# Two PSUM banks for the second layer's output instead of one, in a fused attention and mixture-of-experts kernel

## The chip, the cores and the metric

One core of one Trainium2 chip runs the whole program. The time is the device time of one execution in microseconds (us); of several runs the median counts. The engines are named as the profile names them: PE multiplies matrices, ACT applies functions and copies with a scale, DVE and POOL work on vectors, SP issues most transfers; POOL also issues the scatters whose row addresses are data.

## What is computed

The reference, cut to what matters (4 batches of 11456 rows of 128 numbers, 49 agents, 8 experts with 1024 hidden units):

```python
def sm(a, b):
    s = scale * (a @ b.transpose(0, 2, 1))
    s = s - s.max(-1, keepdims=True)
    e = np.exp(s)
    return e / (e.sum(-1, keepdims=True) + 1e-09)
agent_v = sm(agents, k) @ v
x = (sm(q, agents) @ agent_v).reshape(B * N, 128)

logits = x @ w_gate                      # 45824 x 8
expert_idx = np.argmax(logits, axis=1)
gate_w = softmax(logits)[np.arange(B * N), expert_idx]
for e in range(8):
    rows = expert_idx == e
    y[rows] = np.maximum(x[rows] @ w1[e], 0.0) @ w2[e]
return gate_w[:, None] * y
```

## The kernel before, in words

**Stages.** For each batch, `k_ops` forms the scores of the 49 agents with all keys and their maximum, `v_ops` takes the exponentials and sums the values, which gives agent_v, and `m_ops` multiplies agent_v with each expert's w1 (L640), splits the product into a high and a low fp16 part (ACT at L645, DVE at L648) and stores it in DRAM as `md` (L653). So layer 1 of a token needs only its 49 probabilities: they multiply the 49 rows of `md`.

The 90 blocks of 128 queries of a batch are cut into groups (`GROUPS`, L72, 9 in all, of 16 to 50 blocks). For each group `q_ops` loads queries (`cf` buffers, L376), splits them (L380 on ACT, L384 on DVE), multiplies them with the agents (L399 to L401, into a PSUM tile `misc`), takes the exponentials into `rows` (L694 to L708), transposes them (L723, into `misc`, copied out by ACT at L728) and multiplies them for the router's logits (L737, copied out by ACT at L741). `r_ops` finds each token's expert and place (two matmuls at L800 and L804, the rest on DVE) and writes `tab`, which expert each tile of 128 tokens has (L937 to L960). `row_ops` lets POOL scatter each block of 128 rows to DRAM by place (L972, out is `rows`): one indirect transfer per block, 360 in all.

**Tiles.** `tile_ops` does the experts' part, 372 tiles of 128 tokens of one expert. Four tiles share a load of their rows (`ec` L1030, `rt` L1032). SP stages the tile's weights where the expert changes (`Mst` L1010, `Wst` L1006). PE does layer 1 (16 matmuls, L1041 and L1042) into the PSUM tile `hp`; ACT the relu into `hhi` (L1090); DVE the rest `hlo` (L1094); PE layer 2, 16 matmuls with `hhi` (L1048, L1049) and 8 with `hlo` (L1054), into the PSUM tile `yp`; ACT scales it into `yo` (L1105); POOL scatters the 128 rows to the output (L972, out is `out`). On PE the order is layer 1 of tile i+1, then layer 2 of tile i; on ACT the relu of tile i+1, then yo of tile i.

`w_ops` loads w2 of each expert once (L1138) and splits it into a high part (ACT, L1144) and a low part (DVE, L1147) in `w2s`. Some experts use the fixed load buffers `cf`, some the plain buffers `wf`, some a part of the score buffer S, as `W2CF` and `W2S` say. `m_ops` loads w1 of experts 4 to 6 of the first batch through `wf`.

**PSUM.** Its eight banks hold two `hp` tiles of two banks, three `misc` and one `yp`. `RINGS` (L79) says how many tiles or buffers each name has; a new one waits until the one that it takes the place of is read.

**The order.** Every piece of work is an `op` of `Plan` (L101 to L212) with an engine, a cost in us, a key (about its due time, counted in tiles; negative before the first tile) and what it depends on. `run` takes step by step the engine and the piece that could start first by the costs, then the one with the lowest key, and looks no further ahead than `WINDOW` (for SP, in the early part, `AHEAD0`) beyond the lowest key that is left. The instructions of each engine stand in that order. The constants near the top give keys: `KQ0`, `QK1`, `W1K`, `W2K`, `W2V`, `W2VD` and `PRE1` for the first two groups and the weights, `QAFTER` and `W2L` for behind which load of v a load may go, `R1K` for the row scatters of the second group, and `A2K`, `A3K`, `RATE2` and `RATE` for the start and length of the later groups:

```python
    a = A2K
    for g in GR[2:]:
        end = s0[g.i] - ENDK
        b = end - (RATE2 if g.b == 0 else RATE) * g.nb
...
        row_ops(g, Keys(b, end, g.nb))
        a = b
```

The layer-2 tile and its place in the ring of `yp`:

```python
            x.yp = ps.tile([P, P], F32, name="yp", bufs=RINGS["yp"])
            layer2_hi(x.yp, o, x.hi)
```

Of the kernel before, what the change touches and what calls it, by code (L numbers as in the profile page):

```python
# [41 lines left out]
NS = 4  # L42
SPARE = (2, 1, 1, 1)
CUT, CUT2, KPOOL, VPOOL = (0.18, 0.31, 0.44), 0.33, (), ()
R1K = (-17.6, -0.2)
RATE2, A3K = 0.46, -5.5
RATE = 1.085
ENDK = 8.6
WINDOW = 20.0
SLACK0, SLACK = 0.1, 0.08  # L50
AHEAD0 = 40.0
QK1, A2K = -910.0, -27.3
QAFTER = 3
KQ0 = -964.0
W2L = [8] * 8
W1L = [8] * 8
LDK = 3.3
PRE1 = -20.0
W2CF = (4, 5, 6, 7)

MMC0 = 1.85
FIRSTW, SK0 = 0.5, 900.0
# [1 line left out]
TABK0 = -944.5  # L64
MRING = ("mm", "mm", "mm", "hhi", "hhi", "hlo", "hlo", "mm")
W1S, W2S = (7,), (0, 1, 2)
MK, MKD, W2V, W2VD = -947.5, 0.02, -947.0, 0.3
PRE0K, PRE0 = -966.0, 0
V0POOL = (1, 3, 5, 7)
W1K, W2K = -957.0, -950.0  # L70

GROUPS = [(0, 0, 16), (0, 16, 24), (0, 40, 50), (1, 0, 40), (1, 40, 50), (2, 0, 40), (2, 40, 50), (3, 0, 40), (3, 40, 50)]  # L72
GB = max(n for _, _, n in GROUPS)
# [2 lines left out]

RINGS = {"misc": 3, "hp": 2, "yp": 1, "cf": 4, "chi": 2, "clo": 2, "xs": 2, "ef": 2, "wf": 3, "an": 2, "et": 2, "mm": 3,  # L79
         "rows": 2, "rt": 4, "ec": 3, "hhi": 2, "hlo": 2, "yo": 8, "a16": 2, "af": 2, "ls": 2, "qm": 2,  # L80
         "G": 2, "lg": 2, "sm": 2, "idx": 2, "isig": 2, "bm": 2}

# [18 lines left out]
class Plan:  # L101
# [18 lines left out]
    def run(self, window):  # L120
# [34 lines left out]
        def start(o):  # L155
            t = max(at[o], clk.get(o.eng, 0.0))
            cnt = {}
            for g in o.new:
                r = rings.setdefault(g.ring, [])
                if g in mine and mine[g] != len(r):  # L160
                    return None
                n = RINGS.get(g.ring, 1)
                k = len(r) + cnt.get(g.ring, 0)
# [8 lines left out]
        while left:  # L172
# [4 lines left out]
            for e, L in ready.items():  # L177
                now = clk.get(e, 0.0)
                c = None
                lim = todo[head].key + AHEAD0 if e == "SP" and todo[head].key < -15.0 else limit  # L180
                for o in L:
# [38 lines left out]
def agent_attention_moe(ctx: ExitStack, tc: tile.TileContext, qT, kT, v, agT, wg, w1, w2, out):  # L220
# [10 lines left out]
    def misc(shape, dt=F32):  # L231
        return ps.tile(shape, dt, name="misc", tag="misc", bufs=RINGS["misc"])

    def buf(name, shape, dt=F32, **kw):
        return wk.tile(shape, dt, name=name, bufs=RINGS.get(name, 1), **kw)


    ident = cst.tile([P, P], F16, name="ident")
    make_identity(nc, ident)
    rel = wk.tile([P, P], F32, name="rel", tag="xs", bufs=RINGS["xs"])  # L240
    nc.gpsimd.iota(rel, pattern=[[1, P]], base=0, channel_multiplier=-1,
# [27 lines left out]
    dup = cst.tile([P, A2 + 64], F32, name="dup")  # L269
    tmp = wk.tile([P, P], F32, name="tmp", tag="ef", bufs=RINGS["ef"])  # L270
    nc.vector.tensor_scalar(fold, rel, 0.0, None, op0=OP.is_equal)
# [12 lines left out]
    PW = 2 * P + 1  # L284
    CF = [cst.tile([P, UB // 2 * PW + 1], F32, name=f"cf{i}") for i in range(RINGS["cf"])]
    for t in CF:
# [690 lines left out]
    def prefill_ops(g, key):  # L977
        def go():
            nc.sync.dma_start(g.dram.rearrange("(q p s) c -> p q (s c)", s=4, p=P),
                              padrow.bitcast(I32)[:, None, :].to_broadcast([P, g.nq, 2 * TW]))  # L980
        g.o_pre = dma(None, None, g.nq * 512 * TW * 2, key, fn=go)

    def row_ops(g, key):
        g.o_rows = []
        for k in range(g.nb):
            def go(k=k):
                n = TAIL if g.k0 + k == NBLK - 1 else P
                scat(g.dram.rearrange("r (c o) -> (r c) o", o=1), g.idx[:n, k:k + 1], g.r32[:n, k, :], f"rows{g.i}")
            g.o_rows.append(PL.op("POOL", 1.26, go, key(), [g.o_pre, g.o_idx, g.o_scale, g.o_el[k // g.ub]], nbytes=58000,
                                  use=[g.grow, g.gidx]))  # L990
# [132 lines left out]
    def w_ops(e, lkey, key):  # L1123

        r = Rec()
        ring = "S" if e in W2S else "cf" if e in W2CF else "wf"
        t = BT[0]
# [49 lines left out]
    g0 = GR[0]  # L1177
    q_ops(g0, Keys(KQ0, KQ0 + 2, g0.nb // g0.ub + 1), ring="wf" if g0.ub * P <= F else "cf")
    r_ops(g0, Keys(-949, -948.5, 12), TABK0)
# [4 lines left out]
    for o in g0.o_ld:  # L1184
        o.after = [vl[QAFTER]]
    for o in BT[0].o_mm:
# [3 lines left out]
    g1 = GR[1]  # L1190
    prefill_ops(g1, PRE1)
    q_ops(g1, Keys(QK1, QK1 + 3, g1.nb // g1.ub + 1))
    r_ops(g1, Keys(-60, -59, 12))
    row_ops(g1, Keys(*R1K, g1.nb))
    for o in g1.o_ld:
        o.after = [vl[-1]]
    g1.o_pre.after = [g1.o_ld[-1]]
    for e, a in enumerate(o_ws):
        a.after = [vl[W2L[e]]]
    g0.o_pre.after = [vl[PRE0]]  # L1200
# [5 lines that stand above are left out]
        if g.b == 1 and g.k0 == 0:  # L1206
# [79 lines left out]
```

## Time and profile before

| | us |
|---|---|
| median of 3 runs | 1495.15 (1493.97 to 1502.36) |
| the profiled execution | 1502.17 |
| its span | 1500.3 |
| PE busy | 1166.5 (78%) |
| DVE busy | 845.5 (56%) |
| POOL busy | 832.9 (56%) |
| ACT busy | 752.8 (50%) |

The mean granted clock of PE over the span was 0.931 of full speed. The span is what the profiler saw from the first to the last instruction. A busy time is the sum of an engine's instructions and tells nothing of where the others wait; for that the trace is read by stage. Lines of the form "engine name line <- engine name line" tell what an engine waited for: the total in us, how often, and the longest.

### The profile page before, as it was taken

What the parts mean: (1) busy time and instruction counts of PE and PEld (TensorE: products, weight loads), DVE (VectorE), ACT (ScalarE), POOL (GpSimd) and SP (SyncE); (2) the same over time, 40 slices, a digit from 0 to 9 for tenths busy, and PEclk for the clock granted to TensorE, in tenths of its full rate; (3) what the DMA queues carried; (4) which work ended last, traced back from release to release, by engine and by line L of the source; (5) the groups of instructions that cost most, each with busy time, mean ns of one, the idle gap of its engine ahead of it and who ended that gap; (6) DMA issues with size and microseconds to landing.
All of it is one profiled execution on the core that took longest, in us unless ns stands there. A gap on an engine that the chain in (4) does not pass through costs nothing. (4 is left out here: it accounts for less than half of the span.)

```text
span 1500.3 us, 45968 instructions
## 1 busy us (share of the span) xinstructions
PE 1166.5 (78%) x18670; PEld 1048.5 (70%) x18670; DVE 845.5 (56%) x1269; ACT 752.8 (50%) x1166; POOL 832.9 (56%) x1505
## 2 busy tenths in 40 slices
PE   4743677878777897888877788888887888879995
PEld 3442676667767776767776777777776777769995
DVE  6665594567575645573557545577456333335553
ACT  5542653555544546444554544656453443435663
POOL 1156367555566665665656666557555555664443
PEclk9966788989999999999999998999999999999998
DMA  8989445863352584383263557256131133122210
GB/s 284 321 275 254 130 100 169 239 195 97 110 168 87 162 229 141 81 220 91 63 194 91 147 172 214 73 142 133 42 101 37 40 92 97 40 68 74 48 45 24
DMA packets 236562, 198.40 MB, mean 132 GB/s; under 512 B 121122, under 2 KB 213932, under 8 KB 236320
## 3 DMA queue, kind: packets, MB, share of 16 engines
q1 hardware_dynamic: 212896, 162.15, 38.2%
q0 software_dynamic: 23424, 33.05, 7.6%
q8 instruction: 149, 2.44, 0.7%
q14 instruction: 93, 0.76, 0.2%
HBM read 107.98 MB, written 59.60 MB: 112 GB/s over the span
## 5 line engine op out<-in xcount | busy, mean ns | idle before, releaser
L1094 DVE SCALAR_TENSOR_TENSOR hlo<-hp,hhi 128x1024 f16<-128x1024 f32 x372 | 452.9, 1221 | 441.9 <-ACT hhi L1090 380.8
L972 POOL DMA_INDIRECT out<-yo,rt x372 | 384.6, 1034 | 492.7 <-ACT yo L1105 451.5
L1090 ACT ACTIVATE hhi<-hp 128x1024 f16<-128x1024 f32 x372 | 381.0, 1024 | 240.6 <-PE hp L1042 99.0
L1048 PE MATMUL yp<-Wst,hhi 128*128 128x128 f16 x2976 | 392.7, 224 | 115.2 <-ACT yo L1105 91.9
L972 POOL DMA_INDIRECT rows<-rows,idx x360 | 382.8, 1063 | 124.4 <-issue 84.6
L1041 PE MATMUL hp<-ec,Mst 98*128 98x128 f16 x2976 | 397.4, 223 | 33.0 <-issue 25.3
L1042 PE MATMUL hp<-ec,Mst 98*128 98x128 f16 x2976 | 396.0, 223 | 15.7 <-issue 15.6
L1049 PE MATMUL yp<-Wst,hhi 128*128 128x128 f16 x2976 | 393.2, 224 | 6.9 <-issue 6.7
L1049 PEld LDWEIGHTS <-hhi 128*128 128x128 f16 x2976 | 298.9, 101 | 132.3 <-issue 131.0
L1041 PEld LDWEIGHTS <-Mst 98*128 98x128 f16 x2976 | 296.1, 100 | 49.1 <-issue 40.5
L1042 PEld LDWEIGHTS <-Mst 98*128 98x128 f16 x2976 | 297.5, 100 | 26.5 <-issue 26.1
L1048 PEld LDWEIGHTS <-hhi 128*128 128x128 f16 x2976 | 298.4, 101 | 24.8 <-issue 14.6
L1105 ACT ACTIVATE yo<-yp,rt 128x128 f32<-128x128 f32 x372 | 137.0, 368 | 296.7 <-PE hp L1042 167.0
L1054 PE MATMUL yp<-Wst,hlo 128*128 128x128 f16 x2976 | 244.6, 224 | 31.8 <-issue 20.1
L1054 PEld LDWEIGHTS <-hlo 128*128 128x128 f16 x2976 | 188.3, 100 | 53.5 <-issue 33.5
L384 DVE TENSOR_TENSOR clo<-cf,chi 128x1280 f16<-128x1280 f32 (+1 forms) x71 | 104.6, 1474 | 21.0 <-ACT chi L380 18.0
L401 PE MATMUL misc<-a,clo 128*128 128x49 f16 x720 | 76.2, 192 | 37.6 <-issue 22.0
L380 ACT CAST chi<-cf 128x1280 f16<-128x1280 f32 (+1 forms) x71 | 88.7, 1251 | 28.7 <-PE misc L401 7.3
L399 PE MATMUL misc<-a,chi 128*128 128x49 f16 x720 | 76.4, 193 | 30.8 <-ACT chi L380 20.8
L401 PEld LDWEIGHTS <-clo 128*128 128x128 f16 x720 | 64.1, 102 | 40.6 <-issue 23.2
L399 PEld LDWEIGHTS <-chi 128*128 128x128 f16 x720 | 65.3, 102 | 37.2 <-ACT chi L380 21.9
L400 PE MATMUL misc<-a,chi 128*128 128x49 f16 x720 | 76.5, 193 | 16.5 <-issue 16.3
(176 smaller groups left out, 932.4 us busy)
## 6 DMA issues: line engine op xcount, KB each, us to landing
cf<-in_kT SPq DMA_DIRECT2D x36, 640.0 KB
cf<-in_v SPq DMA_DIRECT2D x36, 640.0 KB
cf<-in_qT SPq DMA_DIRECT2D x32, 640.0 KB
Mst<-md SPq DMA_DIRECT2D x30, 512.0 KB
Wst<-w2s SPq DMA_DIRECT2D x30, 512.0 KB
wf<-in_w SPq DMA_DIRECT2D x28, 512.0 KB
rows<-padrow SPq DMA_DIRECT2D x4, 2304.0 KB
md<-mm SPq DMA_DIRECT2D x56, 128.0 KB
```

The lines of the kernel that those rows point to most:

```text
L384: (nc.gpsimd if pool else nc.vector).tensor_sub(by_pairs(st.lo), st.f, by_pairs(st.hi))
L399: nc.tensor.matmul(p[:, j], h, t.a[:, 0], start=True, stop=False)
L401: nc.tensor.matmul(p[:, j], l, t.a[:, 0], start=False, stop=True)
L972: st = nc.gpsimd.indirect_dma_start(out=dst, out_offset=bass.IndirectOffsetOnAxis(ap=idx, axis=0), in_=src, in_offset=None, **kw)
L1041: nc.tensor.matmul(h_, m[:A2, h, c:c + P], e, start=True, stop=False)
L1042: nc.tensor.matmul(h_, m[:A2, h, 512 + c:512 + c + P], e, start=False, stop=True)
L1048: nc.tensor.matmul(yp, h, w[:, fb * 256 + P:(fb + 1) * 256], start=(fb == 0), stop=False)
L1049: nc.tensor.matmul(yp, h, w[:, fb * 256:fb * 256 + P], start=False, stop=False)
L1054: nc.tensor.matmul(yp, lo[:, fb * P:(fb + 1) * P], w[:, fb * 256:fb * 256 + P], start=False, stop=(fb == FB - 1))
L1090: nc.scalar.activation(x.hi, x.hp, AF.Relu)
L1094: nc.vector.scalar_tensor_tensor(x.lo, x.hp, 0.0, x.hi, op0=OP.max, op1=OP.subtract)
L1105: nc.scalar.activation(x.yo, x.yp, AF.Copy, scale=r.rt[:, o, 1:2].bitcast(F32))
```

## The change

PSUM's eight banks are dealt out anew: `yp` has two tiles and `misc` two. There are six fixed load buffers `cf` instead of four and one plain buffer `wf` instead of three; expert 3's w2 goes through `cf` too. The splits of w2 have keys from -40 on in steps of 2, instead of -947 in steps of 0.3. The w2 loads may go after the seventh load of v instead of the ninth, and the first group's queries after the first load of v. The other constants move the keys of loads, row scatters and later groups. No function is changed.

```diff
--- before.py
+++ after.py
@@ -42,21 +42,21 @@
 NS = 4
 SPARE = (2, 1, 1, 1)
 CUT, CUT2, KPOOL, VPOOL = (0.18, 0.31, 0.44), 0.33, (), ()
-R1K = (-17.6, -0.2)
-RATE2, A3K = 0.46, -5.5
-RATE = 1.085
+R1K = (-17.79, -5.05)
+RATE2, A3K = 0.47, 13.17
+RATE = 0.88
 ENDK = 8.6
 WINDOW = 20.0
 SLACK0, SLACK = 0.1, 0.08
-AHEAD0 = 40.0
-QK1, A2K = -910.0, -27.3
-QAFTER = 3
-KQ0 = -964.0
-W2L = [8] * 8
+AHEAD0 = 68.5
+QK1, A2K = -910, -0.41
+QAFTER = 0
+KQ0 = -968.81
+W2L = [6] * 8
 W1L = [8] * 8
 LDK = 3.3
-PRE1 = -20.0
-W2CF = (4, 5, 6, 7)
+PRE1 = -22.82
+W2CF = (3, 4, 5, 6, 7)
 
 MMC0 = 1.85
 FIRSTW, SK0 = 0.5, 900.0
@@ -64,10 +64,10 @@
 TABK0 = -944.5
 MRING = ("mm", "mm", "mm", "hhi", "hhi", "hlo", "hlo", "mm")
 W1S, W2S = (7,), (0, 1, 2)
-MK, MKD, W2V, W2VD = -947.5, 0.02, -947.0, 0.3
+MK, MKD, W2V, W2VD = -947.5, 0.02, -40, 2
 PRE0K, PRE0 = -966.0, 0
 V0POOL = (1, 3, 5, 7)
-W1K, W2K = -957.0, -950.0
+W1K, W2K = -950.35, -950
 
 GROUPS = [(0, 0, 16), (0, 16, 24), (0, 40, 50), (1, 0, 40), (1, 40, 50), (2, 0, 40), (2, 40, 50), (3, 0, 40), (3, 40, 50)]
 GB = max(n for _, _, n in GROUPS)
@@ -76,7 +76,7 @@
 
 
 
-RINGS = {"misc": 3, "hp": 2, "yp": 1, "cf": 4, "chi": 2, "clo": 2, "xs": 2, "ef": 2, "wf": 3, "an": 2, "et": 2, "mm": 3,
+RINGS = {"misc": 2, "hp": 2, "yp": 2, "cf": 6, "chi": 2, "clo": 2, "xs": 2, "ef": 2, "wf": 1, "an": 2, "et": 2, "mm": 3,
          "rows": 2, "rt": 4, "ec": 3, "hhi": 2, "hlo": 2, "yo": 8, "a16": 2, "af": 2, "ls": 2, "qm": 2,
          "G": 2, "lg": 2, "sm": 2, "idx": 2, "isig": 2, "bm": 2}
```

What it does to the order of the instructions, at three places.

PE, layer 2 of a tile in the middle of the program (`hhi` is the relu's output, `Wst` the staged w2, `yp` the PSUM tile; the names in brackets are semaphores of the engine or queue waited for). Before:

```order
L800 LDWEIGHTS ones
L800 MATMUL misc<-oh,ones 128x400
L804 LDWEIGHTS tri
L804 MATMUL misc<-oh,tri 128x400
L1048 LDWEIGHTS hhi [waits DMAHW0_49,Activation_49]
L1048 MATMUL yp<-Wst_128,hhi 128x128 [waits Activation_49]
L1049 LDWEIGHTS hhi
L1049 MATMUL yp<-Wst_128,hhi 128x128
```

And now:

```order
L1042 MATMUL hp<-ec,Mst_126 128x128
L1048 LDWEIGHTS hhi [waits Activation_49]
L1048 MATMUL yp<-Wst_133,hhi 128x128 [waits DMAHW7_49]
L1049 LDWEIGHTS hhi
L1049 MATMUL yp<-Wst_133,hhi 128x128
```

The weight load waits for the relu in both; the first matmul's wait for ACT, which is the one for `yo` of the tile before, is gone, and what is left on it here is the load of the staged weights.

DVE, the routing table of the first group and the splits of w2 (`tab` is the table, `q` the counts per expert, L648 the low part of agent_v times w1). Before:

```order
L648 SCALAR_TENSOR_TENSOR mm<-misc,mm 128x512
L1147 SCALAR_TENSOR_TENSOR w2s<-cf_109,w2s 128x8x128
L1147 SCALAR_TENSOR_TENSOR w2s<-cf_110,w2s 128x8x128
L1147 SCALAR_TENSOR_TENSOR w2s<-wf,w2s 128x8x128
L937 TENSOR_SCALAR tm<-q_840 1x1
L938 TENSOR_SCALAR jt<-jiota,tm 1x23
L941 TENSOR_TENSOR t_986<-jt,q_840 1x161
L943 TENSOR_REDUCE jt<-t_986 1x23
```

And now:

```order
L937 TENSOR_SCALAR tm<-q_844 1x1
L938 TENSOR_SCALAR jt<-jiota,tm 1x23
L941 TENSOR_TENSOR t_922<-jt,q_844 1x161
L943 TENSOR_REDUCE jt<-t_922 1x23
L949 TENSOR_TENSOR jt<-jt 1x22
L958 MEMSET jt 1x1
L959 SCALAR_TENSOR_TENSOR jt<-jt 1x23
L960 CAST tab_134<-jt 1x2x23
L962 TENSOR_SCALAR ovff<-q_844 1x1
L648 SCALAR_TENSOR_TENSOR hhi<-hp,hhi 128x512
L1147 SCALAR_TENSOR_TENSOR w2s<-S,w2s 128x8x128 x3
L648 SCALAR_TENSOR_TENSOR mm<-misc,mm 128x512
```

The table stood behind all eight splits of w2 and stands ahead of them now.

SP, the loads for the first tiles (`ec` and `rt` are the rows of the first four tiles, `Mst` and `Wst` the staged weights). Before:

```order
L1016 TENSOR_LOAD tab_130
L1010 ISA
L1010 DMA Mst_125<-md_118 128x1x2048
L1030 DMA_TRANSPOSE ec<-rows_133 128x512
L1032 DMA rt<-rows_133 128x4x2
L1006 ISA
L1006 DMA Wst_127<-w2s 128x2048
```

And now:

```order
L653 DMA md_122<-hlo 64x1024 x4
L1030 DMA_TRANSPOSE ec<-rows_137 128x512
L1032 DMA rt<-rows_137 128x4x2
L1016 TENSOR_LOAD tab_134
L1010 ISA
L1010 DMA Mst_126<-md_122 128x1x2048
```

The rows of the first tiles were loaded behind the fourth `Mst`; now they are ahead of the first one.

## Rows read from the trace of the kernel before

**Rows 1.** Busy times by stretch; columns as in the first line.
```profile
core 0: us, PE busy (x) PEld busy (x) DVE busy (x) ACT busy (x) POOL busy (x), PEclk, DMA share, GB/s
71.60:122.80 51.20, 20.72 (x300) 17.55 (x296) 38.64 (x86) 25.03 (x40) 24.41 (x41) 0.66 0.93 263
...
200.00:1350.00 1150.00, 929.67 (x14764) 829.41 (x14762) 642.73 (x926) 571.59 (x895) 697.08 (x1250) 0.95 0.45 124
1350.00:1486.00 136.00, 133.42 (x2368) 132.58 (x2367) 72.41 (x61) 82.49 (x120) 64.04 (x123) 1.00 0.21 52
```
**Rows 2.** Timeline, ACT, 1399 to 1406 us: start, length, instruction, idle before it.
```profile
1400.52 0.37 ACT L1105 ACTIVATE yo<-yp,rt 128x128 f32<-128x128 f32 x1 [0.32 <-PE yp L1054]
...
1402.76 0.37 ACT L1105 ACTIVATE yo<-yp,rt 128x128 f32<-128x128 f32 x1 [0.32 <-PE yp L1054]
```
**Rows 3.** Groups by line, 1250 to 1340 us: count | busy, mean ns | idle before.
```profile
L972 POOL DMA_INDIRECT rows<-rows,idx x25 | 24.1, 964 | 7.0 <-issue 7.0
L1054 PE MATMUL yp<-Wst,hlo 128*128 128x128 f16 x223 | 17.9, 219 | 2.0 <-issue 2.0
```
**Rows 4.** Timeline, POOL, 120 to 160 us: the second group's row scatters.
```profile
122.89 0.96 POOL L972 DMA_INDIRECT rows<-rows,idx  x1 [8.34 <-DVE tm L937]
...
140.56 0.96 POOL L972 DMA_INDIRECT rows<-rows,idx  x1 [0.23 <-issue]
...
141.82 0.96 POOL L972 DMA_INDIRECT rows<-rows,idx  x1 [0.22 <-issue]
...
154.46 0.96 POOL L972 DMA_INDIRECT rows<-rows,idx  x1 [0.23 <-issue]
```
**Rows 5.** Timeline, PE, in the same stretch.
```profile
141.62 0.20 PE L400 MATMUL misc<-a,chi 128*128 128x49 f16 x1 [0.78 <-issue]
143.04 0.20 PE L401 MATMUL misc<-a,clo 128*128 128x49 f16 x1 [1.22 <-issue]
```
**Rows 6.** Timeline, ACT, in the same stretch.
```profile
159.96 1.02 ACT L1090 ACTIVATE hhi<-hp 128x1024 f16<-128x1024 f32 x1 [15.93 <-remote]
```
**Rows 7.** Groups by line, whole program.
```profile
L972 POOL DMA_INDIRECT rows<-rows,idx x360 | 382.8, 1063 | 124.4 <-issue 84.6 <-DVE mm L648 30.6 <-DVE tm L937 8.3
L399 PE MATMUL misc<-a,chi 128*128 128x49 f16 x720 | 76.4, 193 | 30.8 <-ACT chi L380 20.8 <-issue 9.5 <-DVE xs L698 0.5
L728 ACT COPY et<-misc 98x640 f16<-98x640 f16 (+1 forms) x74 | 49.7, 682 | 30.7 <-remote 12.1 <-PE misc L723 10.0 <-PE hp L1042 7.6
L648 DVE SCALAR_TENSOR_TENSOR mm<-misc,mm 128x512 f16<-128x512 f32 x26 | 17.8, 685 | 12.2 <-ACT mm L645 7.2 <-issue 5.0
L1147 DVE SCALAR_TENSOR_TENSOR w2s<-cf,w2s 128x1024 f16<-128x1024 f32 x4 | 4.8, 1213 | 0.0
```
**Rows 8.** Waits, whole program: us in total, times, longest us.
```profile
ACT hhi L1090 <- PE hp L1042: 99.0, 96, 3.4
PE yp L1048 <- ACT yo L1105: 91.9, 115, 2.4
```
**Rows 9.** Waits, 1250 to 1340 us.
```profile
ACT hhi L1090 <- PE hp L1042: 20.4, 9, 3.3
...
PE yp L1048 <- ACT yo L1105: 6.1, 10, 1.5
```
**Rows 10.** Timeline, ACT and PE, 1270 to 1290 us: one tile.
```profile
1270.63 1.02 ACT L1090 ACTIVATE hhi<-hp 128x1024 f16<-128x1024 f32 x1 [3.34 <-PE hp L1042]
...
1271.55 0.36 ACT L1105 ACTIVATE yo<-yp,rt 128x128 f32<-128x128 f32 x1
...
1271.96 0.22 PE L1048 MATMUL yp<-Wst,hhi 128*128 128x128 f16 x1 [0.45 <-ACT yo L1105]
```
**Rows 11.** Timeline, SP, POOL and PE, 86 to 104 us: the beginning.
```profile
86.88 2.81 SPq L1010 DMA_DIRECT2D Mst<-md  x3
...
95.70 0.09 POOL L433 MEMSET spacer<- 1x1 f32 x1
...
98.72 1.24 SPq L1030 DMA_TRANSPOSE ec<-rows  x1
...
102.64 0.31 PE L1041 MATMUL hp<-ec,Mst 98*128 98x128 f16 x1
```

## The prediction

> **What bounds the kernel now.** I read the busy times by stage first. From 1350 to 1486 us PE is busy for 133.42 of 136 us at a granted clock of 1.00 [rows 1]: after the last row scatter the tiles run alone, at PE's own rate. Its length there is the distance of two yo drains, 1402.76 − 1400.52 = 2.24 us per tile [rows 2]. From 200 to 1350 us PE is busy for 929.67 of 1150 us, POOL for 697.08, DVE for 642.73, ACT for 571.59 and the DMA engines for 0.45 [rows 1]: nothing is full, so the losses lie in how engines follow each other. That stretch holds three quarters of the time.
>
> A clean piece of it is 1250 to 1340 us: 223 layer-2 rest matmuls at 8 per tile are 27.9 tiles, and there are 25 row scatters [rows 3]. At 2.24 us the tiles need 62.5 of the 90 us; 27.5 us are lost, 1.1 us per row scatter. What a row scatter does to PE is plainest where 24 of them follow each other, from 122.89 to 154.46 us, most of them 1.26 us apart [rows 4]: PE then issues a matmul or two and stands for 1.22 us, a gap that the profile gives to "issue", no wait that it can name [rows 5], and a relu comes 15.93 us late [rows 6]. Of the 360 row scatters [rows 7], 16 belong to the first group and 24 are these; the other 320 cost, at 1.1 us, about 352 us. This is the largest loss in the kernel, and the change takes away none of these scatters.
>
> The chain of one tile on PE is layer 1 of the next tile, layer 2 hi, layer 2 lo; ACT does the next relu, then drains yp into yo. With one yp bank, layer 2 of the next tile cannot begin until yo has read the bank. Over the program that wait is 91.9 us in 115 waits; ACT's relu waits longer for layer 1, 99.0 us in 96 waits [rows 8]. In the clean piece the two are 6.1 us in 10 waits and 20.4 us in 9 [rows 9].
>
> **The change, part by part.**
> *Two banks for layer 2's output.* In the changed order 1 layer-2 matmul waits for ACT's yo where 366 did (the overflow code's included). So up to 91.9 us is there to win. The lower bound is nothing: one tile shows why. Its relu starts at 1270.63 us after 3.34 us of waiting for layer 1, runs 1.02 us, yo follows behind it on ACT at 1271.55 and layer 2 starts at 1271.96 after a wait of 0.45 [rows 10]. Without the wait it could start at the relu's end, 1271.65: 0.31 us of 0.45 is won, and then the relu is last. When signals are late they are late for both: the relu has slack for PE's work of one tile less its own time, 2.24 − 1.02 = 1.2 us, and it waits for up to 3.4 us in the rows [rows 8]. And in the clean piece only 6.1 of the 27.5 lost us stand as this wait; a PE that is ahead by 0.3 us still meets the next row scatter's 1.1 us. Between 0 and 91.9 I take a third, nearer to the lower end because the relu's waits in the clean piece are three times as large as yo's: **−31 us**.
>
> A page speaks for more. The Trainium skill, "Perfetto Trace Analysis", Optimizing Tensor Performance, says that independent matmul groups should rotate through PSUM banks so that one's drain runs beside the next one's matmuls. By that rule the whole wait would go, and the sum would be 61 us lower; the row on the relu that is late beside it is why I don't take that. Against the change speaks "TensorE: Matmul & The Clock Gate" of the Trainium skill, where PSUM double-buffering of a warm matmul with few rows gave 126.6 to 125.5 us, next to nothing; by it this term would be close to 0, and no run here shows which holds.
>
> *Two banks for scores and the like instead of three.* Matmuls into misc that wait for a drain (L399, L640, L723, L737, L800, L804) go from 52 to 109 in the order, 57 more, most at L723 (20 to 39), L737 (7 to 27) and L399 (8 to 19). Below, each costs nothing: 8 such waits stand at L399 now, and the trace gives them 0.5 us of its 30.8 [rows 7]. Above, each costs one drain, 0.68 us (L728 682 ns, L648 685 ns [rows 7]), 57 × 0.68 = 39 us. I take a quarter of a drain, 0.17 us, because the row of L399 is nearest: **+10 us**. Behind each such matmul PE's tile matmuls stand, so the price is on the path; who waits then is the relu.
>
> *The beginning.* Now POOL ends the first group's row scatters at 95.70, the loads of its rows go out at 98.72 and the first layer 1 runs at 102.64 [rows 11]. In the changed order the first routing table is ahead of the w2 splits on DVE, and SP issues the loads of the rows ahead of the first Mst load, which was issued from 86.88 us in the old order. That load, 2.81 us for three [rows 11], now comes behind: +1 to +3 us, and at worst +8 if the table is late too. On the other side POOL stands 8.34 us before the second group's rows at 122.89, waiting for DVE [rows 4]; if the earlier routing removes half of it, −4 us; with all of it and a first tile that is 4 us sooner, −12 us. I take **−5 us**, more than half of that gap less what the loads cost.
>
> *Six cf buffers, one wf buffer, w2 by its keys.* All eight w2 splits still stand ahead of the first tile's rest (hlo) on DVE, though fewer stand ahead of the table; a split takes 1.21 us [rows 7] and DVE is busy for 38.64 of 51.20 us from 71.60 to 122.80 [rows 1], while the first group's 16 row scatters run. Cover: those scatters. With one wf buffer the w1 loads of experts 4 to 6 go one behind the other, each after PE's use of the one before; a load of 512 KB at the stage's 263 GB/s [rows 1] is 2.0 us, so two more steps are some 4 us beside that cover. If the cover is gone they delay the md store, then the Mst load, and are part of the +8 above. Later q and k loads come earlier; the DMA engines are at 0.45, so I count **0**.
>
> *The keys of the row scatters.* There are as many; they stand among the outputs of 273 tiles instead of 289, the groups start later and the last one comes at the same tile, the 312th. If a scatter costs what it costs, nothing changes: **0**. If a tile beside scatters costs 90 ÷ 27.9 = 3.2 us however many stand there, 16 tiles at 1.0 us are −16 us.
>
> Sum: −31 + 10 − 5 = **−26 us** against the profiled execution of 1502.2 us, 1476. That execution stands 7.0 us above the median of the runs, 1495.15, so I state 1495.15 − 26 = 1469, rounded to **1468 us**. With a third to two thirds of the yo wait, the misc price at its two ends and the start's bounds, the case itself spans 1440 to 1487.
>
> **The rivals.**
> *The whole wait goes.* For it: layer 2 then needs only the relu, which ACT does before yo, and L1048's wait is the largest single wait of PE. Against: the relu's 3.34 us. Time: 1495 − 92 + 10 − 5 = 1408 us, and 1426 if a fifth of the 92 comes back at the relu. It is also what the bank rotation rule of the Trainium skill, named above, would give. Chance 0.17.
> *The wait only moves.* Row scatters set the pace; PE stops in layer 1 or at the relu for the time that it no longer stands at yo. For it: gaps at "issue" that no bank explains [rows 5] and the 1.1 us per scatter. The 31 us don't come, the +10 and −5 stay: 1495 + 5 = 1500 us, and with cheap misc waits 1490. Chance 0.18.
> *Slower: the misc bank costs more than the yp bank gives.* A score matmul that waits for a drain on ACT or DVE blocks the tile matmuls behind it on PE, and that drain itself waits for a PE signal that is as late as the relu's. For it: 20.8 of L399's 30.8 us are already waits on ACT [rows 7]. Against: PE could be in a stall at that moment anyway. Its gain stays at 31 + 5 = 36 us, so it decides from 36 ÷ 57 = 0.63 us per wait on; at 1 us the time is 1495 − 36 + 57 = 1516 us. Chance 0.15.
> *The change doesn't do what it says:* the w2 parts still stand ahead of the first tile's rest, so that part does nothing or adds DVE work just when the first tile starts, at 8 us on a gain that doesn't come: 1503 us or more. Chance 0.02.
>
> **How the numbers follow.** The forecast has 0.48. The range reaches from 1412, which leaves out the better half of the first rival, to 1505, which leaves out most of the slower one: about 0.2 outside. A measurement of this kernel can tell about 0.5% (7.5 us) from no change. Faster: 0.48 + 0.17 = 0.65. Same: the wait that only moves, 0.18. Slower: 0.15 + 0.02 = 0.17.
>
> **What would show it.** Right: L1048's wait for yo is gone from the waits; the relu's wait for layer 1 grows by some 40 to 60 us; a piece of tiles with row scatters holds about 29 tiles in 90 us instead of 27.9; L399, L723 and L737 wait for ACT and DVE by 5 to 20 us more; tiles after the last scatter still take 2.24 us; the second group's row scatters start some 4 us earlier than at 122.89. Wrong: the yo wait is gone and the number of tiles per 90 us is unchanged (it moved), or 33 and more (it was all real); or the misc waits grow by over 36 us.

## The result and the profile after

The change made the kernel slower: 1513.1 us median of 4 runs against 1497.9 of 4, a ratio of 1.0105 (95% interval 1.0063 to 1.0147). The forecast was 1468 us. The profiled execution took 1512.4 us, its span is 1510.6.

Busy times by stretch in the profile after; the columns are those of [rows 1].

```profile
71.60:122.80 51.20, 25.98 (x270) 19.39 (x268) 37.92 (x86) 19.24 (x33) 26.14 (x40) 0.60 0.72 233
200.00:1350.00 1150.00, 954.88 (x14651) 856.24 (x14651) 639.44 (x927) 570.59 (x888) 688.11 (x1240) 0.91 0.45 122
1350.00:1486.00 136.00, 130.34 (x2302) 128.88 (x2303) 69.99 (x58) 79.93 (x116) 63.95 (x122) 1.00 0.23 51
```

From 200 to 1350 us PE issued 14651 matmuls where it was 14764 [rows 1], yet was busy for 954.88 us instead of 929.67: the granted clock of the stretch is 0.91, not 0.95. The clock has two levels here, 2.4 and 1.2 GHz; by the clock records of the two traces the stretch has 208 us at 1.2 GHz, in 40 spells, where it had 110 us in 21. A matmul cost 65.2 ns of busy time instead of 63.0, 32 us for all of them. The forecast had no term for this.

The waits of the same stretch, total us, times and longest, in the kernel before:

```profile
PE yp L1048 <- ACT yo L1105: 90.0, 112, 2.4
PE hp L1041 <- issue: 25.0, 59, 1.1
PE yp L1054 <- issue: 20.1, 48, 1.1
PE hp L1042 <- issue: 15.2, 40, 1.1
```

and after:

```profile
PE hp L1042 <- issue: 39.6, 88, 1.2
PE hp L1041 <- issue: 36.3, 69, 1.2
PE yp L1054 <- issue: 33.3, 62, 1.6
```

The wait of layer 2 for yo is gone, as planned. But PE's idle time fell by only 25 us (1150 − 929.67 = 220 before, 1150 − 954.88 = 195 after). In the three other groups of matmuls shown, 49 us came back as "issue" gaps (60.3 before, 109.2 after), the kind of gap that stands under POOL's scatters [rows 4, 5]; all of PE's "issue" gaps together went from 112 to 155 us, so of the 90 us 43 came back in this form. Over the program, the relu's wait for layer 1 rose from 99.0 us [rows 8] to:

```profile
ACT hhi L1090 <- PE hp L1042: 154.1, 132, 4.4
```

How an "issue" gap is paid for twice shows in 15 us of the profile after. The busy times:

```profile
1290.00:1295.00 5.00, 4.85 (x84) 4.54 (x82) 2.45 (x2) 2.67 (x4) 3.29 (x7) 1.00 0.24 58
1295.00:1300.00 5.00, 1.82 (x24) 1.19 (x22) 0.33 (x1) 1.02 (x1) 3.36 (x8) 0.87 0.15 30
1300.00:1305.00 5.00, 4.98 (x48) 5.00 (x49) 2.12 (x2) 1.76 (x3) 2.82 (x5) 0.50 0.07 22
```

and the timeline of POOL and of PE in the middle of it:

```profile
1295.46 0.96 POOL L972 DMA_INDIRECT rows<-rows,idx  x1 [0.22 <-issue]
1296.72 0.99 POOL L972 DMA_INDIRECT out<-yo,rt  x1 [0.23 <-issue]
1298.01 0.96 POOL L972 DMA_INDIRECT rows<-rows,idx  x1 [0.25 <-issue]
...
1298.59 0.22 PE L1041 MATMUL hp<-ec,Mst 98*128 98x128 f16 x1 [1.15 <-issue]
1300.02 0.28 PE L1041 MATMUL hp<-ec,Mst 98*128 98x128 f16 x1 [1.16 <-issue]
```

While scatters follow each other PE gets 24 matmuls done in 5 us instead of 84. Then the clock is granted at 0.50, which is 1.2 GHz: the next 5 us are full, with 48 matmuls. The stop loses 60 matmuls and the low clock behind it another 36, and no wait shows the second loss.

The clean piece from 1250 to 1340 us, by groups, after:

```profile
L1048 PE MATMUL yp<-Wst,hhi 128*128 128x128 f16 x216 | 31.0, 234 | 0.1
L972 POOL DMA_INDIRECT rows<-rows,idx x26 | 25.1, 965 | 6.2 <-issue 6.2
L1054 PE MATMUL yp<-Wst,hlo 128*128 128x128 f16 x217 | 18.9, 230 | 3.3 <-issue 2.9 <-DVE hlo L1094 0.4
```

and by busy time:

```profile
1250.00:1340.00 90.00, 74.34 (x1084) 68.63 (x1084) 33.07 (x27) 35.85 (x54) 54.53 (x105) 0.89 0.20 47
```

It is the lesson in small: L1048's idle time went from 9.6 us (6.1 of them for yo [rows 9]) to 0.1, and yet the piece holds 217 ÷ 8 = 27.1 tiles with 26 row scatters, fewer than the 27.9 with 25 [rows 3]. PE's idle time fell by 3.3 us, but its clock is 0.89 where it was 1.00, and a matmul costs 68.6 ns instead of 64.7, 4.2 us in all:

```profile
1250.00:1340.00 90.00, 71.08 (x1099) 62.99 (x1097) 33.60 (x28) 36.17 (x55) 54.41 (x105) 1.00 0.19 49
```

(the same stretch of the kernel before).

The beginning, from the timelines of SP, PE and POOL after:

```profile
96.05 1.24 SPq L1030 DMA_TRANSPOSE ec<-rows  x1
...
98.85 2.82 SPq L1010 DMA_DIRECT2D Mst<-md  x3
...
102.92 0.29 PE L1041 MATMUL hp<-ec,Mst 98*128 98x128 f16 x1 [1.00 <-DMA Mst<-md]
...
119.18 0.96 POOL L972 DMA_INDIRECT rows<-rows,idx  x1 [1.61 <-DVE ovff L962]
```

The rows of the first tiles load 2.7 us earlier, Mst behind them, and layer 1 starts at 102.92 us instead of 102.64; POOL's gap ahead of the second group is 1.61 us instead of 8.34 and that group starts 3.7 us earlier [rows 4, 11]. The ends of each tile's yo, worked out from the traces (tiles are counted from 0), show how long this advantage lasted (PSUM alone, and PSUM with the start's keys and buffers, are experiments below):

| yo of tile | before | after | PSUM alone | PSUM and start |
|---|---|---|---|---|
| 4 | 169.5 | 165.1 | 170.4 | 166.8 |
| 52 | 395.8 | 392.9 | 397.9 | 412.4 |
| 196 | 969.8 | 953.3 | 958.7 | 981.8 |
| 276 | 1234.5 | 1238.7 | 1215.8 | 1247.3 |
| 371 | 1485.7 | 1495.3 | 1468.5 | 1500.3 |

At tile 4 both have 40 row scatters behind them, so the 4.4 us there are real. At tile 52 after has 98 and before 104, at tile 196 it is 256 and 265: the lead of 2.9 us and most of the 16 us are work put off, and at tile 276 after is behind.

### The profile page after: what moved, and what is told of

Read it like the earlier page. It is cut to its first block, busy times and chain, and to the rows that moved or that the text cites. A ratio compares the mean times of both kernels' runs of the same rounds, so it can differ in the third digit from the quotient of the medians.

```text
span 1510.6 us, 45646 instructions
## 1 busy us (share of the span) xinstructions
PE 1204.1 (80%) x18670; PEld 1082.8 (72%) x18670; DVE 845.1 (56%) x1269; ACT 755.2 (50%) x1166; POOL 829.5 (55%) x1507
## 5 line engine op out<-in xcount | busy, mean ns | idle before, releaser
L1041 PE MATMUL hp<-ec,Mst 98*128 98x128 f16 x2976 | 422.8, 230 | 53.4 <-issue 39.1
L1042 PE MATMUL hp<-ec,Mst 98*128 98x128 f16 x2976 | 420.6, 229 | 40.1 <-issue 39.6
L1048 PE MATMUL yp<-Wst,hhi 128*128 128x128 f16 x2976 | 410.4, 229 | 21.0 <-issue 13.6
L1049 PE MATMUL yp<-Wst,hhi 128*128 128x128 f16 x2976 | 409.0, 228 | 12.0 <-issue 11.4
L1041 PEld LDWEIGHTS <-Mst 98*128 98x128 f16 x2976 | 306.3, 103 | 76.8 <-issue 63.9
L1042 PEld LDWEIGHTS <-Mst 98*128 98x128 f16 x2976 | 307.2, 104 | 51.6 <-issue 51.1
L1048 PEld LDWEIGHTS <-hhi 128*128 128x128 f16 x2976 | 304.4, 103 | 35.8 <-issue 24.0
L1049 PEld LDWEIGHTS <-hhi 128*128 128x128 f16 x2976 | 305.9, 103 | 18.8 <-issue 18.1
L1054 PE MATMUL yp<-Wst,hlo 128*128 128x128 f16 x2976 | 256.6, 229 | 53.1 <-issue 35.8
L1054 PEld LDWEIGHTS <-hlo 128*128 128x128 f16 x2976 | 196.2, 103 | 79.2 <-issue 48.6
L380 ACT CAST chi<-cf 128x1280 f16<-128x1280 f32 (+1 forms) x71 | 88.8, 1251 | 60.4 <-remote 26.5
L399 PE MATMUL misc<-a,chi 128*128 128x49 f16 x720 | 78.0, 195 | 26.8 <-issue 13.5
L400 PE MATMUL misc<-a,chi 128*128 128x49 f16 x720 | 78.1, 195 | 10.8 <-issue 10.6
L399 PEld LDWEIGHTS <-chi 128*128 128x128 f16 x720 | 66.8, 103 | 25.8 <-issue 13.3
```

The costliest lines, as they stand in the source:

```text
L399: nc.tensor.matmul(p[:, j], h, t.a[:, 0], start=True, stop=False)
L1041: nc.tensor.matmul(h_, m[:A2, h, c:c + P], e, start=True, stop=False)
L1042: nc.tensor.matmul(h_, m[:A2, h, 512 + c:512 + c + P], e, start=False, stop=True)
L1048: nc.tensor.matmul(yp, h, w[:, fb * 256 + P:(fb + 1) * 256], start=(fb == 0), stop=False)
L1049: nc.tensor.matmul(yp, h, w[:, fb * 256:fb * 256 + P], start=False, stop=False)
L1054: nc.tensor.matmul(yp, lo[:, fb * P:(fb + 1) * P], w[:, fb * 256:fb * 256 + P], start=False, stop=(fb == FB - 1))
```

## Experiments

The change has three parts that can be put in alone: P, the PSUM banks (`RINGS`: misc 2, yp 2); R, the keys of the later groups (`RATE`, `RATE2`, `A2K`, `A3K`); S, all the rest (the early keys, six `cf`, one `wf`). Theories: A, the second yp bank itself brings little, because PE's stops move and the clock falls oftener; B, the keys undo a gain that is there; C, the lost misc bank costs what the yp bank gives. From the second set of runs on, the letters mean what the text of each expectation says, mostly R (A) and S (B) as what spoils P.

One thing has to be known for all of them: the kernel before takes about 1500 us on some chips and 1201 to 1205 us on others. Runs made together share a chip, and ratios are only compared within one kind.

**P, and all but P, on a chip of the 1500 us kind.**

```diff
-RINGS = {"misc": 3, "hp": 2, "yp": 1, "cf": 4,
+RINGS = {"misc": 2, "hp": 2, "yp": 2, "cf": 4,
```

> The kernel before with only the PSUM banks dealt out anew (two for yp, two for misc); the planner then orders by these. A, the loss lies in the second yp bank itself (PE runs ahead, then stops at the relu for longer at a time, and the granted clock falls more often): 0 to +15 us against before, L1048 waits for yo no more, the granted clock from 200 to 1350 us near 0.91 as after and not 0.95 as before. B, the loss lies in the keys (row scatters of the later groups stand closer): about -30 us, the clock stays at 0.95. C, the third misc bank is what is missed: the yo gain of 30 and a loss of up to 39, 0 to +10 us, with L399, L723 and L737 waiting on DVE and ACT by 30 us more.

> The change without its PSUM part (yp one bank, misc three; all keys and load buffers changed). A: -5 to 0 us against before (only the start is gained), clock 0.95 from 200 to 1350 us. B: +20 to +40 us, since the 30 us of the yp bank are missing and the crowded keys remain, clock 0.91. C: -5 to 0 us.

P alone: 1489.9 us against 1499.4, ratio 0.9931 (0.9898 to 0.9963): faster. All but P: 1.0024 (0.9989 to 1.006), no difference. So P's gain is there, smaller than forecast, and the parts don't add: 0.9931 and 1.0024 would make 0.9955, and the whole change is 1.0105. None of A, B or C expected both numbers.

**The same order, only the banks.** The planner still orders by one yp and three misc; only the real number of banks is changed.

```diff
-    return ps.tile(shape, dt, name="misc", tag="misc", bufs=RINGS["misc"])
+    return ps.tile(shape, dt, name="misc", tag="misc", bufs=2)
...
-            x.yp = ps.tile([P, P], F32, name="yp", bufs=RINGS["yp"])
+            x.yp = ps.tile([P, P], F32, name="yp", bufs=2)
```

The run for misc alone has the first edit only.

> The order planned as before, yp one bank, misc two banks (one bank of PSUM unused): the price of the lost misc bank alone. A and B: 0 to +8 us. C: +15 to +39 us with misc waits that account for it.

> The order planned as before (with one yp and three misc), but two real banks for yp and two for misc, so instructions stand as before and only the waits differ. A: -5 to +10 us, yo wait gone, the relu's wait for layer 1 up by 40 us or more, clock under 0.93 from 200 to 1350 us. B: -30 us, clock 0.95. C: +0 to +15 us, the misc waits up by 30 us, clock 0.95.

Two misc banks alone: 1.0074 (1.0039 to 1.0109), 11 us. With two yp banks as well: 1.0021 (0.9978 to 1.0064). The second yp bank is therefore worth 0.5%, 8 us, with instructions in the order of before. The two intervals overlap, but the two sets of ten runs, compared with each other, differ by 9.1 us in the mean (95% interval 3 to 15): the sign is clear, the size rough. From 200 to 1350 us, misc alone:

```profile
200.00:1350.00 1150.00, 925.62 (x14695) 827.95 (x14696) 643.76 (x930) 572.50 (x891) 693.71 (x1241) 0.95 0.44 124
```

its waits there:

```profile
ACT hhi L1090 <- PE hp L1042: 91.6, 72, 5.4
PE yp L1048 <- ACT yo L1105: 88.6, 111, 3.2
```

and with two yp banks:

```profile
200.00:1350.00 1150.00, 959.10 (x14793) 859.40 (x14794) 644.92 (x930) 572.79 (x895) 688.67 (x1250) 0.92 0.45 124
```

with this wait of the relu, and none of L1048 for yo:

```profile
ACT hhi L1090 <- PE hp L1042: 108.0, 87, 4.0
```

This is the cleanest reading of the case. Nothing moved but a wait of 88.6 us, which is gone. PE's idle time fell from 224 to 191 us, so 33 of the 88.6 us are won as idle time. But its busy time rose by 33 us, of which 27 is price (63.0 to 64.8 ns a matmul); the clock went from 0.95 to 0.92, by the clock records from 112 us at 1.2 GHz in 27 spells to 192 us in 43. The lost misc bank costs more than A and B allowed (8 us) and less than C did (15); A's clock is there, with a small gain left and the relu's wait up by 16 us, or 26 against before, and not by 40.

The misc bank's price can be seen as waits. Misc alone, whole program:

```profile
L399 PE MATMUL misc<-a,chi 128*128 128x49 f16 x720 | 75.0, 193 | 44.8 <-ACT et L728 19.1 <-ACT chi L380 10.2 <-DVE jt L938 9.5
L723 PE MATMUL misc<-ident,rows 128*98 128x128 f16 x360 | 36.9, 240 | 12.2 <-ACT et L728 5.4 <-issue 2.0 <-DVE rows L708 1.5
```

L399 reads nothing of `et`; L728, the copy into `et`, frees the bank that L399 writes. In the kernel before none of L399's 30.8 us is a wait for it [rows 7]; here one wait of 18.9 us, between 123 and 200 us, is nearly all of the 19.1. In the profiled executions misc alone is 3.7 us behind before at tile 4, 8.3 at tile 52 (104 row scatters behind both) and 7.7 at the end, so most of this price is paid early.

**P with R, and P with S.**

> PSUM dealt out anew and the keys of the later groups (A2K, A3K, RATE, RATE2); start, weights and load buffers as before. PSUM alone was 1489.9, all but PSUM 1503.5, everything 1513.1. A, the later groups' keys spoil the gain (their row scatters come closer and later, with a PE that no yo wait holds back the clock falls oftener): 1505 to 1518 us, low clock from 200 to 1350 us near the 0.91 of after, the loss between tiles 228 and 311. B, the start's keys and load buffers spoil it: 1485 to 1495 us.

> PSUM dealt out anew with the start's keys, weights' keys and load buffers; the later groups' keys as before. A: 1483 to 1492 us, the 4 us of the earlier start on top of PSUM alone. B: 1505 to 1518 us.

> Only the later groups' keys, one yp bank, three misc. A: 1502 to 1512 us against about 1499.4 of before: the crowded scatters cost something already, less than with two yp banks. B: 1496 to 1503 us.

> Only the start's keys, weights' keys and load buffers. A: 1493 to 1498 us, the start 4 us earlier at tile 4 and nothing else. B: 1500 to 1512 us.

These runs, and the next two sets, fell on chips of the other kind. There all parts lose: R 1.0048 (1.0024 to 1.0073), S 1.0087 (1.0058 to 1.0117), P with R 1.0088 (1.0059 to 1.0118), P with S 1.0156 (1.0115 to 1.0197). The repeats:

> PSUM alone. Where before takes 1500 us: -0.7% as before. Where it takes 1205 us: A, the yo wait is not there to win on that chip and the misc bank costs: +0.3 to +0.8%; rival, the second yp bank gains everywhere: -0.3% or better.

> The change as it is, beside its parts on one chip. On a chip on which before takes about 1500 us: +1.0% against before, as recorded. On one like the last (before 1204.6 us): +1.5 to +2.2%, if the parts add up there (PSUM +0.4 to +0.7, later keys +0.5, start +0.9).

> PSUM and the later groups' keys. Where before takes 1500 us: A (later keys spoil the gain) +0.4 to +1.2% with the loss from tile 228 on; B (the start spoils it) -0.9 to -0.3%. Where it takes 1205 us: +0.9% as in the last call.

> PSUM and the start. Where before takes 1500 us: A -1.1 to -0.5%; B +0.4 to +1.2%. Where it takes 1205 us: +1.6% as in the last call.

P 1.0092 (1.0061 to 1.0123), the whole change 1.0119 (1.0081 to 1.0157), P with R 1.0114 (1.006 to 1.0167), P with S 1.0164 (1.0122 to 1.0207). P costs a little more than A's +0.3 to +0.8% and its rival has fallen; the whole change costs less than the sum of its parts. And with the misc bank alone:

> The order of before, misc two banks, yp one. Where before takes about 1500 us: +0.7% as measured. Where it takes 1203 us: the lost misc bank is most of what PSUM alone costs there (+0.9%): +0.5 to +1.0%; if the second yp bank were what costs there: -0.2 to +0.3%.

Misc alone 1.0108 (1.0065 to 1.0151); on the same chip the whole change 1.0121 (1.0055 to 1.0187), P with R 1.0074 (1.0047 to 1.0101), P with S 1.0182 (1.0137 to 1.0228), where +1.2, +1.0 and +1.6% were expected. So on this kind of chip P costs no more than the lost misc bank alone. The second yp bank at the old order was not run there; nothing of a gain by it can be seen. Why shows in the waits: the program of misc alone, the same on both kinds, waits 94.1 us for yo on the first and 10.8 on the second. The profile of R alone (one yp bank, three misc) says more. Its wait for yo, over the program:

```profile
PE yp L1048 <- ACT yo L1105: 10.7, 11, 2.4
```

its tiles beside row scatters, from 970 to 1046 us, by groups:

```profile
L972 POOL DMA_INDIRECT rows<-rows,idx x29 | 27.9, 963 | 7.0 <-issue 7.0
L1054 PE MATMUL yp<-Wst,hlo 128*128 128x128 f16 x264 | 20.1, 219 | 0.0
```

and by busy time:

```profile
970.00:1046.00 76.00, 74.57 (x1332) 74.28 (x1330) 40.72 (x34) 46.04 (x67) 60.56 (x117) 1.00 0.39 102
```

264 ÷ 8 = 33 tiles in 76 us are 2.30 us a tile, with 29 row scatters beside them: the scatter takes POOL as long as before (963 ns against 964 [rows 3]), but PE doesn't feel it. Of 10.7 us of waiting, at the share that was kept above (8 of 88.6), 1 us would be won (an estimate).

**P with S where before takes 1500 us.** Only the fourth run fell on such a chip.

> PSUM and the start, later groups' keys as before. Where before takes about 1500 us: A (the later keys undo the gain of PSUM) -1.1 to -0.5%, mean clock 0.91 or higher; B (the start undoes it) +0.4 to +1.2%, clock near 0.90. Where it takes 1203 us: +1.7% as in the two runs before.

1518.5 us against 1496.1, ratio 1.0158 (1.0111 to 1.0204). So S undoes P's gain there, against 0.9931 for P without S (on another chip of the kind). R isn't needed for that: with R added the whole change is at 1.0105. Whether R alone would undo it too was not measured on this kind. The start's advantage is real (tile 4 in the table above), and it is lost again by tile 52, where P with S is 14.5 us behind P with as many row scatters done (104 and 105). How it is lost stands in the stretch from 200 to 1350 us, P first, then P with S:

```profile
200.00:1350.00 1150.00, 960.68 (x15172) 857.57 (x15173) 653.39 (x925) 587.62 (x918) 698.32 (x1265) 0.94 0.46 126
200.00:1350.00 1150.00, 940.76 (x14607) 833.55 (x14604) 635.18 (x918) 567.22 (x886) 684.33 (x1234) 0.93 0.44 122
```

PE is idle for 209 us instead of 189, and a matmul costs 64.4 ns instead of 63.3, 16 us for all of them. One stop can be named: from 289 to 295 us L640 waits 5.5 us for L728, which frees its misc bank, and the clock falls to 0.50 at that place. Neither P nor all but P has such a wait, but it is a small part of the 32 us between the two, and the whole change, which lacks it too, is still slow.

**P with S's buffers only.**

```diff
-RINGS = {"misc": 3, "hp": 2, "yp": 1, "cf": 4,
+RINGS = {"misc": 2, "hp": 2, "yp": 2, "cf": 6,
...
-"wf": 3,
+"wf": 1,
```

> PSUM dealt out anew and only the load buffers of the start's part (six cf, one wf); all keys as before. Where before takes about 1500 us: A, the buffers bring the loss of the start's part (it grows along the whole program, as it did from tile 36 to 311, since w1 and the queries of every batch go through them): +0.7 to +1.7%; B, the early keys bring it: -1.1 to -0.3%, as PSUM alone. Where it takes 1203 us: A +1.4 to +1.8%; B +0.6 to +1.1%.

It fell on the other kind: 1.011 (1.0072 to 1.0149), between P (1.0092) and P with S (1.0156 to 1.0182) and nearer to P, at the upper end of B. There the early keys are likely most of S's cost (the intervals overlap, and the chips differ); on the 1500 us kind this wasn't settled.

## Why the prediction was wrong

**Which step failed: the term for two yp banks, −31 us, and with it the adding up of terms.** At unmoved order the bank gave 8 us; with the planner's order P as a whole gave 0.7%, 10 us, where −31 + 10 made −21. The step "a third of the wait" counted only what comes back as waiting, and as idle time a third of it was indeed won, 33 of 88.6 us. What comes back as slower matmuls, 27 us at the same order, was not in the sum. The prediction had the granted clock in its rows, 0.95 from 200 to 1350 us [rows 1], and never asked what the clock would do when PE's pauses move.

The larger share of the miss is the adding up. The forecast was −26 us, the change measured +16. Of these 42 us, 11 lie in P (−21 forecast, −10 measured) and 9 in R and S without P (−5 forecast, +4 measured, not clear of nothing). About 22 us are left that arise only when the parts are put together; the sum had no term for them, and P with S shows that S beside P is enough to bring them.

**What of it was right.** The yo wait went; the relu's wait for layer 1 grew by 55 us (40 to 60 was forecast); tiles alone are at 2.24 us still (two yo start at 1421.69 and 1423.93); the second group's scatters start 3.7 us earlier (4 was forecast). The price of the lost misc bank, +10, measured 11 us on one kind of chip and 13 on the other. That the size came out so well is in part luck: it was reckoned as 57 waits of 0.17 us, and in the run that measures it one wait of 18.9 us is most of what came on top; idle time at L399, L723 and L737 is 42.6 us before, 62.0 with misc alone and, in the planner's new order, 51.1 after. Not all the signs came true: these three lines were to wait for ACT and DVE by 5 to 20 us more in the change, and they went from 30.0 to 31.6 us; and the piece from 1250 to 1340 us was to hold 29 tiles and holds 27.1. The rows of L723 and L737 before:

```profile
L723 PE MATMUL misc<-ident,rows 128*98 128x128 f16 x360 | 36.1, 236 | 5.4 <-DVE rows L708 2.7 <-issue 2.2 <-DVE rl L546 0.2
L737 PE MATMUL misc<-G,et 98*128 98x17 f16 x360 | 16.6, 172 | 6.4 <-ACT et L728 4.5 <-DVE G L583 1.1 <-issue 0.7
```

and all three after:

```profile
L399 PE MATMUL misc<-a,chi 128*128 128x49 f16 x720 | 78.0, 195 | 26.8 <-issue 13.5 <-ACT chi L380 9.7 <-ACT ls L741 2.2
L723 PE MATMUL misc<-ident,rows 128*98 128x128 f16 x360 | 35.8, 236 | 11.7 <-ACT et L728 6.3 <-DVE rows L708 3.5 <-issue 0.8
L737 PE MATMUL misc<-G,et 98*128 98x17 f16 x360 | 16.8, 173 | 12.6 <-ACT et L728 7.3 <-issue 3.7 <-DVE G L583 1.1
```

**The start, −5, and the keys, 0.** At tile 4 the gain is 4.4 us, about as forecast. It doesn't reach the end: S and R together, without P, give +0.2% (not clear of nothing), and beside P they turn 0.9931 into 1.0105. A term read at the beginning was carried to the end as if nothing between could take it back.

**The rivals.** The slower one gave 1516 us and the time is 1513, but its mechanism isn't what was measured, and that it came so near is luck: it needed 0.63 us for each of 57 new waits, and the misc bank costs 11 ÷ 57 = 0.2. The row that spoke for it doesn't do so either: the 20.8 us that L399 waits for ACT are waits for `chi`, its own input (L380), not for a bank. "The wait only moves" is nearest to the mechanism, 43 us of "issue" gaps, and it lacked the clock. That the whole wait would be won has fallen: the bank rotation rule of the Trainium skill, "Perfetto Trace Analysis", Optimizing Tensor Performance, holds in that the drain now runs beside the next matmuls, and 88.6 us of wait gave 8.

**Two slips in the sum.** 1495.15 − 26 is 1469, and 1468 was stated. And the bounds that are named (31 to 61 us of the yo wait, 0 to 39 for misc, −12 to +8 for the start) give 1422 to 1511 us, not 1440 to 1487: by its own bounds the change was nearer to a loss than the text said.

**What stays open.** Why S costs so much beside P on the 1500 us kind, by its early keys or its buffers; the one run that was to tell fell on the other kind. What R does beside P on that kind. And why the clock falls more often when PE is less idle: the rows show one fall while PE stood under scatters (1295 to 1300 us), and the same order with the yo wait gone has 43 falls instead of 27. The second bank doesn't bring as much of it in every order: P in the planner's order has 30 falls and 63.3 ns a matmul. That more uneven work is the reason was not tried by itself.

## What to carry to other kernels

A wait on the busiest engine can be worth much less than its total (8 of 88.6 us here): ask where the engine stops next and at what clock it then runs, and compare busy time per instruction, not only waits, in the profile after. Buffers that are traded within one memory have two prices, and the one on the losing side (11 us here) is as real as the one on the winning side. Parts whose constants were set together need not add up (here 22 us were in the putting together): test them together, on the chip for which they are meant.

## What was not expected of the hardware

The same program takes 1500 us on some chips and 1203 on others. From 125 to 150 us, while POOL scatters the second group's rows, the program of misc alone does this on the first kind:

```profile
125.00:150.00 25.00, 9.43 (x145) 8.53 (x143) 12.14 (x27) 6.77 (x8) 20.50 (x35) 0.64 0.95 285
```

and the same program this on the second, with 18 row scatters in the 25 us on both:

```profile
125.00:150.00 25.00, 19.18 (x384) 18.21 (x383) 22.35 (x33) 22.46 (x37) 21.04 (x37) 0.89 1.01 325
```

POOL is busy alike (20.5 and 21.0 us), and PE, ACT and DVE are busy about two to three times as long; PE issues 384 matmuls instead of 145. The stall of other engines under indirect transfers, 1.1 us each, which was the largest loss in the forecast's reading, belongs to the first kind of chip; the runs don't show what differs between the chips.

On the first kind PSUM alone is the fastest version measured (0.9931); on the second no version that ran beat the kernel before.
